# A fused attention and two feed-forward layers in one kernel: the first two blocks' loads, high parts and step order

## The chip, the cores and the metric

One Trainium2 chip, one core. The metric is the device time of one execution in microseconds; with several runs, their median. All operands come from HBM and the result goes back there. TensorE multiplies, VectorE and ScalarE do the elementwise work, GpSimd some of it, and SyncE issues the DMAs. "Local" and "strided" below are the two kinds of attention heads.

## The reference

Three stages, one behind the other, in fp32, over 2304 tokens (4 sequences of 576) and 512 channels:

```python
# attention: q, k, v are (4, 8, 576, 64); heads 0-3 local, heads 4-7 strided
rel = pos[:, None] - pos[None, :]
mask_local = (rel >= 0) & (rel < 32)
mask_strided = (rel >= 0) & (pos[None, :] % 32 == pos[:, None] % 32)
scores = where(mask, q @ k.T / 8, -1e9); attn = softmax(scores); out = attn @ v
# first feed-forward, w_in 512x2048, w_out 2048x512
h = x @ w_in; x = (h - tanh(h)) @ w_out
# second, w_gate and w_val 512x1536, w_out 1536x512
xn = x / sqrt(mean(x*x) + 1e-6) * rms_g
out = (silu(xn @ w_gate) * (xn @ w_val)) @ w_out
```

## The kernel before, in words

The tokens are cut into nine blocks of 256, gathered in five groups (two blocks, two, one, two, two). For a group the kernel computes the attention of its blocks and then the first feed-forward layer, 16 steps over f of 128 hidden channels each: a product with `w_in` (`pe_h`), tanh, a subtraction, and a product with `w_out` (`pe_x`) that is summed in PSUM. While a group's feed-forward runs, the attention of the next group is worked in between. The second feed-forward layer comes after all that.

Precise products take two parts of each operand: a high part, which is the value rounded for TensorE, and a low part, which is what is left. A product is then three matmuls. A weight of 128x512 arrives packed in 8-byte words and goes through four steps: `scale` (word **A** in the list below: ScalarE reads the raw weight), `merge` (**B**: two VectorE steps put the bits together), `high` (**P**: a cast, line 203) and `low` (**Q**: VectorE subtracts the high part). Weights are numbered in the order in which they are loaded: 0 is `in` 0, 1 is `in` 1, 2 is `out` 0, 3 is `in` 2, 4 is `out` 1; below they are in0, in1, out0, in2, out1.

The start, the attention of blocks 0 and 1 and the first three units of the feed-forward, is not left to the planner: the string `START` (line 25) lists every step by hand, and `first` (line 1212) issues them in that order. Each engine takes its own steps strictly in the order of the list; between engines only the data's semaphores order them. The words are these, with a block's number and L (local) or D (strided), and after it a half (0 or 1) or PSUM banks:

- the first word, after `<`: the loads, one letter each, issued on SyncE's queue in this order: t the table (a 128x544 tile: `ident16` and masks for the early blocks in columns 0 to 191, the identity in 192 to 319, masks of later blocks in 320 to 543), a and A the local queries and keys of block 0 and 1 (512 KB), b and B the strided ones (512 KB), c and C the local values (384 KB, on 96 partitions), d and D the strided values (256 KB), w the next weight (512 KB), 2 the loads of block 2;
- W9: nine products of zeros on TensorE at the very start;
- s: scores on TensorE, into two of the four banks x; m: row maxima on VectorE (line 447); e: exponentials on ScalarE (line 461); n: division by the sums on VectorE (lines 469 to 471); p: transposes on TensorE; c: their copy out of PSUM on ScalarE (line 487); v: the product with the values on TensorE; y: high part of the result on ScalarE (line 490); z: its low part on VectorE (line 494). So e1D0 is the exponentials of block 1, strided heads, half 0;
- h, T, G, I, J, X: a feed-forward unit: the product with `w_in` on TensorE, tanh on ScalarE, the subtraction on VectorE, the high part on ScalarE, the low part on VectorE, the product with `w_out` on TensorE. Unit 0 is f = 0 on block 0, unit 1 f = 1 on block 0, unit 2 f = 0 on block 1. h0 needs Q0 and all z of block 0; h1 needs Q1; h2 all z of block 1; X0 needs J0 and Q2.

Two tiles hold the output of A and two that of B, so a third weight's steps wait for the first's. The strided heads of blocks 0 and 1 take one transpose step and one copy (p0D, c0D) for both halves. What is not in the list is ordered by the planner, which places work by its own estimates of the times and may fill gaps with it; from the second group on the order on TensorE and SyncE is fixed by the program.

Of the kernel before, what the change touches and what calls it, by code (L numbers as in the profile page):

```python
# [22 lines left out]


START = """
<tabcdwABwCDwww2ww
W9 s0Lx m0L0 e0L0 m0L1 s0Dx n0L0 e0L1 m0D0 p0L0m1 m0D1 s1Lx A0 e0D0 B0 c0L0a n0L1 p0L1h1 P0 Q0 m1L0 m1L1 e0D1 c0L1a
v0Lh0 s1Dx n0D1 n0D0 A1 e1L0 p0Dh1 e1L1 y0L1 n1L0 m1D0 m1D1 c0Da n1L1 v0Dm0m1 y0L0 e1D0 y0D1 z0L0 y0D0 z0L1 p1L0h1
c1L0a B1 z0D0 P1 z0D1 p1L1h1 e1D1 c1L1a Q1 n1D0 n1D1 h0h0 A2 v1Lm1 T0 B2 A3 G0 y1L0 p1Dh1 c1Da y1L1 B3 v1Dh1m0 I0 P2
J0 y1D1 z1L0 y1D0 h1h0 T1 z1L1 z1D1 z1D0 P3 h2h1 Q2 G1 A4 Q3 T2 B4 I1 G2 J1 I2 J2 X0  # L30
"""


# [1 line left out]
def attn_moe_moe_kernel(  # L35
# [24 lines left out]
    nc = tc.nc  # L60
# [60 lines left out]
    tab = one.tile([128, 544], F32, name="tab")  # L121
# [27 lines left out]
    def mm(out_, lhsT, rhs, start, stop):  # L149
        nc.tensor.matmul(out_, lhsT, rhs, start=start, stop=stop, skip_group_check=True)  # L150
# [3 lines left out]
    def room_of(i):  # L154
        return (held, "v") if i >= 2 * FA - HELD else (wts, "w")

    class Weight:
# [40 lines left out]
            )  # L198
            self.b = t.bitcast(F32)

        def high(self, pool, tag):
            self.t = pool.tile([128, 2, 4, 128], F32R, tag=tag, name="w")
            nc.scalar.copy(out=self.t[:, 0].rearrange("p c f -> p (c f)"), in_=self.b)

        def low(self, eng):
            t = self.t.rearrange("p s c f -> p s (c f)")
# [40 lines left out]
    for f in range(1, FA):  # L247
# [3 lines left out]
    st1 = Stream(  # L251
        [w1[w] for w in w1_order],
        lambda i: room_of(i) + (nc.vector,),
        3, 2 * FA, lambda i: True,
    )
# [244 lines left out]
    class Local(Heads):  # L500
        w = 96
# [340 lines left out]
    def pe_h(g, f, a, e, bank=None):  # L842
        pool, tag = (ps_m, "m") if g == NG - 1 and f % 2 else (ps_h, "h")
        ps = bank("ps_h") if bank else pool.tile([128, 512], F32, tag=nth(tag, 2), name="ps_h")
        ps = ps[:, :e - a]
        w, x = w1["in", f].t, xs[g]
        seq = [(i, k, c) for c in range(4) for i, k in ((0, 0), (0, 1), (1, 0))]
        for n, (i, k, c) in enumerate(seq):
            mm(ps, w[:, i, c, :], x[:, k, c, a:e], n == 0, n == len(seq) - 1)
        h_of[g, f, a] = ps  # L850
# [326 lines left out]
    new_x(0)  # L1177
    new_x(1)

    def tab_load():  # L1180
        nc.sync.dma_start(out=tab, in_=tabs)

    units = [(0, f, 0, SUB) for f in range(LB)]
    for f in range(LB, FA):
# [3 lines left out]
    units += [(g, f, 0, width[g]) for g in range(1, NG) for f in range(FA)]  # L1188

    loads = {  # L1190
        "t": tab_load, "w": lambda: st1.load_to(st1.n + 1),
        **{c: o.load_qk for c, o in zip("aAbB", loc[:2] + strd[0] + strd[1])},
        **{c: o.load_v for c, o in zip("dD", strd[0] + strd[1])},
        **{c: (lambda o=o: o.load_v(0)) for c, o in zip("cC", loc[:2])},
# [6 lines left out]
    def bank_of(tags):  # L1201
        if tags == "x":
            return bank_x
        tags = [tags[k:k + 2] for k in range(0, len(tags), 2)]

        def bank(name):
            tag = tags.pop(0)
            return {"h": ps_h, "m": ps_m}[tag[0]].tile([128, 512], F32, tag=tag, name=name)

        return bank  # L1210

    def first(word):

        op, rest = word[0], word[1:]
        if op == "<":
            for c in rest:
                loads[c]()
        elif op == "W":
            z = att.tile([128, 512], F32, tag="sm", name="zero").bitcast(BF16)[:, :512]
            nc.vector.memset(z, 0.0)  # L1220
            ps = bank_of("m0")("ps_w")
            for _ in range(int(rest)):
                mm(ps, z[:, :128], z, True, True)
        elif op in "ABPQ":
            w = st1.ws[int(rest)]
            pool, tag, e = st1.place(int(rest))
            if op == "A":
                w.scale()
            elif op == "B":
                w.merge()  # L1230
                st1.i = int(rest) + 1
            elif op == "P":
                w.high(pool, tag)
            else:
                w.low(e)
        elif op == "h":
            pe_h(*first_units[int(rest[0])], bank_of(rest[1:]))
        elif op in "TGIJX":
            u = first_units[int(rest)]
            {"T": act_tanh, "G": dve_g, "I": g_hi, "J": g_lo, "X": pe_x}[op](*u)  # L1240
            if op == "J":
                xq.append(u)
            if op == "X":
                xq.remove(u)
        else:
            j, kind, rest = int(rest[0]), rest[1], rest[2:]
            o = loc[j] if kind == "L" else strd[j][0]
            fn = getattr(o, "st_" + op)
            if op in "sv":
                fn(bank_of(rest))  # L1250
            elif op == "p":
                i = 0 if o.fused else int(rest[0])
                fn(i, bank_of(rest if o.fused else rest[1:]))
            elif op == "c":
                fn(0 if o.fused else int(rest[0]), nc.scalar.copy)
            else:
                fn(int(rest))
# [23 lines left out]
    with tc.manual_schedule():  # L1281
        for word in START.split():
            first(word)
# [122 lines left out]
    for j in range(NJ):  # L1406
        for p in range(NP):
            first, last, end = (j, p) == (0, 0), p == NP - 1, (j, p) == (NJ - 1, NP - 1)
            me, nxt = pairs[p], pairs[(p + 1) % NP]
            st = Stage(j, p)  # L1410
# [132 lines left out]
```

## Time and profile before

| | us |
|---|---|
| median of 3 runs | 888.29 |
| lowest and highest | 886.44, 888.67 |
| the profiled execution, its own time | 887.14 |
| its span, first to last instruction | 885.3 |

The profile is of one execution. Its page gives each engine's busy time and the granted clock of TensorE; views by stretch, by engine in order of time and by line or tile show which instruction ran when, and behind it in brackets how long the engine had stood idle and what ended that. Starts are microseconds from the span's start. An instruction's time there may overlap the next one's by some 0.1 us, since the engines work in pipelines.

### The profile page before, as it was taken

How to read it: one execution, taken by the hardware profiler on the slowest of the kernel's cores; microseconds unless marked ns; L12 is line 12 of the kernel's file. 1: busy time of each engine (PE TensorE's matmuls, PEld its weight loads, DVE VectorE, ACT ScalarE, POOL GpSimd, SP SyncE). 2: the span in 40 equal slices, each digit the busy share in tenths (PEclk: the TensorE clock that was granted, in tenths of full speed). 3: DMA queues.
4: the chain of work that ended last, by engine and by line, in shares of the span. 5: the costliest groups of instructions: out<-in, count | busy, mean ns of one | idle time of the engine just before them, and what ended most of it. 6: DMA issues, size and time to landing. Idle time of an engine off the chain costs nothing.

```text
span 885.3 us, 14070 instructions
## 1 busy us (share of the span) xinstructions
PE 865.6 (98%) x5091; PEld 723.4 (82%) x5091; DVE 626.1 (71%) x1290; ACT 413.7 (47%) x916; POOL 247.6 (28%) x309
## 2 busy tenths in 40 slices
PE   7999999999999999999997999999999999999998
PEld 4888888888998887888887977888888888888886
DVE  5999778888779887657779845469688553435544
ACT  6887633323543333778657544533325324322230
POOL 0000057694366853000000449956200000000000
PEclk7999999999999999999999999999999999999999
DMA  9965224221313000889976889866661289544002
GB/s 302 367 221 180 76 75 157 98 63 36 116 55 110 25 19 26 330 311 366 412 262 226 302 304 410 329 239 214 212 216 48 82 315 348 182 147 140 1 1 95
DMA packets 63749, 164.12 MB, mean 185 GB/s; under 512 B 10112, under 2 KB 21760, under 8 KB 63680
## 3 DMA queue, kind: packets, MB, share of 16 engines
q1 hardware_dynamic: 62528, 162.18, 52.2%
q10 hardware_dynamic: 1152, 1.05, 0.3%
q8 instruction: 40, 0.66, 0.3%
q14 instruction: 29, 0.24, 0.1%
HBM read 119.16 MB, written 44.04 MB: 184 GB/s over the span
## 4 chain that ended last, share of the span: by engine, by line
PE 60%; DVE 9%; POOL 7%; issue 2%; DMA 2%; ACT 1%; ACTq 0%; SPq 0%; DVEq 0%; POOLq 0%
PE ps_pr L150 21%; PE ps_o L150 15%; PE ps_x L150 9%; PE ps_h L150 9%; POOL pr L674 5%; DVE so L714 4%; PE ps_q L150 4%; PE ps_m L150 1%; POOL pr L707 1%; DMA raw<-in_w_val_dram 1%; DVE tg L859 1%; DVE g L870 1%; DMA x2d<-xe 1%; DVE sm L450 0%; DMA sq<-in_q_str_dram 0%
## 5 line engine op out<-in xcount | busy, mean ns | idle before, releaser
L150 PE MATMUL ps_h<-xs,w 128*128 128x512 f32 (+1 forms) x984 | 214.3, 366 | 0.7 <-DVE tg L859 0.7
L150 PE MATMUL ps_x<-g,w 128*128 128x512 f32 (+1 forms) x984 | 214.1, 366 | 0.0
L150 PEld LDWEIGHTS ps_h<-xs,w 128*128 128x128 f32 x984 | 169.7, 190 | 30.5 <-DVE tg L859 1.2
L150 PEld LDWEIGHTS ps_x<-g,w 128*128 128x128 f32 x984 | 168.5, 189 | 30.3 <-ACT g L865 0.4
L150 PE MATMUL ps_pr<-xt,wt 128*128 128x512 f32 x576 | 137.0, 390 | 0.5 <-DVE s L1096 0.5
L150 PE MATMUL ps_o<-wt,p 128*128 128x512 f32 x576 | 135.9, 389 | 0.0
L150 PEld LDWEIGHTS ps_pr<-xt,wt 128*128 128x128 f32 x576 | 107.9, 188 | 23.6 <-DVE s L1096 0.9
L150 PEld LDWEIGHTS ps_o<-wt,p 128*128 128x128 f32 x576 | 108.1, 188 | 22.4
L674 POOL TENSOR_TENSOR pr<-sk,sq 128x256 f32<-128x256 f32 (+2 forms) x101 | 83.1, 857 | 132.2 <-DMA sq<-in_q_str_dram 127.8
L865 ACT CAST g<-tg 128x512 fp32r<-128x512 f32 (+1 forms) x82 | 46.5, 567 | 101.2 <-DVE tg L859 100.9
L1117 ACT COPY u<-ps_pr 128x512 f32<-128x512 f32 x72 | 41.9, 587 | 102.8 <-PE ps_pr L150 102.8
L707 POOL TENSOR_TENSOR pr<-sv,se 128x288 f32<-128x288 f32 (+12 forms) x104 | 69.7, 691 | 57.4 <-DVE so L714 19.8
L1169 DVE SCALAR_TENSOR_TENSOR osum<-ps_o,osum 128x512 f32<-128x512 f32 x80 | 54.8, 687 | 26.6 <-PE ps_o L150 25.9
L714 DVE TENSOR_REDUCE so<-pr 128x16 f32<-128x272 f32 (+11 forms) x104 | 64.8, 651 | 8.9 <-POOL pr L707 8.6
L302 POOL TENSOR_TENSOR ws<-wa 128x256 f32<-128x256 f32 x24 | 20.4, 872 | 179.6 <-DVE w L207 155.6
L150 PE MATMUL ps_pr<-xt,wo 128*128 128x512 f32 x288 | 67.4, 389 | 0.0
L150 PEld LDWEIGHTS ps_pr<-xt,wo 128*128 128x128 f32 x288 | 54.1, 188 | 11.2
L870 DVE TENSOR_TENSOR g<-tg,g 128x512 fp32r<-128x512 f32 (+1 forms) x82 | 55.2, 674 | 10.4 <-ACT g L865 9.8
L859 DVE SCALAR_TENSOR_TENSOR tg<-ps_h,tg 128x512 f32<-128x512 f32 (+1 forms) x82 | 50.5, 617 | 15.8 <-ACT tg L854 15.8
L196 DVE SCALAR_TENSOR_TENSOR ct<-ca,ct 128x512 uint32<-128x512 uint32 x68 | 47.5, 706 | 18.9 <-ACT ca L186 18.4
L854 ACT ACTIVATE tg<-ps_h 128x512 f32<-128x512 f32 (+1 forms) x82 | 44.2, 540 | 35.5 <-PE ps_h L150 35.4
L679 DVE TENSOR_REDUCE sc<-pr 128x4 f32<-128x256 f32 (+2 forms) x101 | 43.7, 436 | 12.1 <-POOL pr L674 11.6
(123 smaller groups left out, 1041.1 us busy)
## 6 DMA issues: line engine op xcount, KB each, us to landing
wt<-w SPq DMA_DIRECT2D x84, 512.0 KB, 4.6
w<-w SPq DMA_DIRECT2D x36, 512.0 KB, 6.2
raw<-in_w_out_dram SPq DMA_DIRECT2D x28, 512.0 KB, 6.1
w<-wo SPq DMA_DIRECT2D x24, 512.0 KB, 7.1
raw<-in_w_in_dram SPq DMA_DIRECT2D x16, 512.0 KB, 9.2
raw<-in_w_gate_dram SPq DMA_DIRECT2D x12, 512.0 KB, 7.0
raw<-in_w_val_dram SPq DMA_DIRECT2D x12, 512.0 KB, 7.4
v<-ct SPq DMA_DIRECT2D x24, 256.0 KB, 5.3
```

The costliest lines, as they stand in the source:

```text
L150: nc.tensor.matmul(out_, lhsT, rhs, start=start, stop=stop, skip_group_check=True)
L196: nc.vector.scalar_tensor_tensor(out=t, in0=self.a.bitcast(U32), scalar=3, in1=t, op0=ALU.logical_shift_left, op1=ALU.bitwise_or)
L674: nc.gpsimd.tensor_tensor(out=pr, in0=self.k[:, a:e, :], in1=self.q[:, c - c0:c - c0 + 1, :].to_broadcast([128, e - a, D]), op=ALU.mult,)
L679: pend.append(lambda: nc.vector.tensor_reduce(out=s[:, c - c0, a:e], in_=pr, axis=AX.X, op=ALU.add))
L707: nc.gpsimd.tensor_tensor(out=pr, in0=self.v[:, 0:c + 1, a:e], in1=self.e[:, c - c0, 0:c + 1].unsqueeze(2).to_broadcast([128, c + 1, e - a ...
L714: pend.append(lambda: nc.vector.tensor_reduce(out=o[:, c - g0, a:e], in_=pr.rearrange("l c d -> l d c"), axis=AX.X, op=ALU.add))
L854: nc.scalar.activation(out=t, in_=h_of[g, f, a], func=ACTF.Tanh, scale=WS)
L859: nc.vector.scalar_tensor_tensor(out=t, in0=h_of.pop((g, f, a)), scalar=WS, in1=t, op0=ALU.mult, op1=ALU.subtract)
L865: nc.scalar.copy(out=t[:, 0], in_=t_of[g, f, a])
L870: nc.vector.tensor_tensor(out=t[:, 1], in0=t_of.pop((g, f, a)), in1=t[:, 0].bitcast(F32), op=ALU.subtract)
L1117: nc.scalar.copy(out=u, in_=x[kd])
L1169: nc.vector.scalar_tensor_tensor(out=o, in0=ps, scalar=WS, in1=o, op0=ALU.mult, op1=ALU.add)
```

## The change

It touches the first two blocks alone. The table is loaded in two pieces, columns 0 to 319 (T) first and columns 320 to 543 (M) behind the first weight. The local queries and keys of block 1 (A) are loaded third instead of seventh, ahead of the strided ones of block 0 (b); the values of block 0 (c, d) move behind the first weight. The high parts (P) of the first four weights are cast by GpSimd instead of ScalarE; all later ones stay on ScalarE. The steps stand in another order throughout; some PSUM banks of transposes change with it (p0L0 takes m0, for one). The set of steps is the same.

```diff
 START = """
-<tabcdwABwCDwww2ww
-W9 s0Lx m0L0 e0L0 m0L1 s0Dx n0L0 e0L1 m0D0 p0L0m1 m0D1 s1Lx A0 e0D0 B0 c0L0a n0L1 p0L1h1 P0 Q0 m1L0 m1L1 e0D1 c0L1a
-v0Lh0 s1Dx n0D1 n0D0 A1 e1L0 p0Dh1 e1L1 y0L1 n1L0 m1D0 m1D1 c0Da n1L1 v0Dm0m1 y0L0 e1D0 y0D1 z0L0 y0D0 z0L1 p1L0h1
-c1L0a B1 z0D0 P1 z0D1 p1L1h1 e1D1 c1L1a Q1 n1D0 n1D1 h0h0 A2 v1Lm1 T0 B2 A3 G0 y1L0 p1Dh1 c1Da y1L1 B3 v1Dh1m0 I0 P2
-J0 y1D1 z1L0 y1D0 h1h0 T1 z1L1 z1D1 z1D0 P3 h2h1 Q2 G1 A4 Q3 T2 B4 I1 G2 J1 I2 J2 X0
+<TaAbwMcBdwCDwww2ww
+W9 s0Lx m0L1 m0L0 s0Dx e0L1 m0D0 e0L0 m0D1 n0L1 s1Lx A0 n0L0 p0L1m0 B0 e0D0 e0D1 m1L0 P0 s1Dx n0D0 c0L1a m1L1 p0L0m0
+A1 n0D1 Q0 e1L0 p0Dm1 B1 m1D0 c0L0a e1L1 c0Da A3 m1D1 n1L0 v0Lh0 P1 v0Dm0m1 e1D0 y0D0 y0D1 y0L1 p1L0h1 n1L1 z0D1 z0D0
+y0L0 e1D1 A2 p1L1m0 c1L0a z0L1 z0L0 n1D0 h0h0 c1L1a n1D1 T0 B2 G0 p1Dh1 c1Da v1Lm1 I0 Q1 y1L0 v1Dh1m0 J0 y1L1 P2 y1D0
+y1D1 B3 h1h0 z1L1 z1L0 P3 z1D0 z1D1 T1 Q2 A4 h2h1 G1 T2 Q3 B4 X0 G2 I1 I2 J1 J2
 """
@@ Weight.high
-        def high(self, pool, tag):
+        def high(self, pool, tag, copy=nc.scalar.copy):
             self.t = pool.tile([128, 2, 4, 128], F32R, tag=tag, name="w")
-            nc.scalar.copy(out=self.t[:, 0].rearrange("p c f -> p (c f)"), in_=self.b)
+            copy(out=self.t[:, 0].rearrange("p c f -> p (c f)"), in_=self.b)
@@ the table's load
-    def tab_load():
-        nc.sync.dma_start(out=tab, in_=tabs)
+    def tab_load(a, e):
+        nc.sync.dma_start(out=tab[:, a:e], in_=tabs[:, a:e])
@@ the loads by letter
-        "t": tab_load, "w": lambda: st1.load_to(st1.n + 1),
+        "T": lambda: tab_load(0, 320), "M": lambda: tab_load(320, 544), "w": lambda: st1.load_to(st1.n + 1),
@@ first
             elif op == "P":
-                w.high(pool, tag)
+                w.high(pool, tag, nc.gpsimd.tensor_copy)
```

## Rows read from the trace of the kernel before

**Rows 1.** The page, busy us, share of the span and instructions of TensorE
```profile
PE 865.6 (98%) x5091; PEld 723.4 (82%) x5091; DVE 626.1 (71%) x1290; ACT 413.7 (47%) x916; POOL 247.6 (28%) x309
```
**Rows 2.** Busy time by stretch; last three columns: clock, DMA share, GB/s
```profile
0.00:22.00 22.00, 16.13 (x253) 10.09 (x253) 11.96 (x47) 13.61 (x63) 0.54 (x8) 0.77 0.93 301
22.00:66.00 44.00, 42.08 (x417) 36.03 (x396) 41.87 (x123) 37.98 (x106) 0.00 (x0) 0.96 0.82 294
```
**Rows 3.** TensorE in order of time: start, us, instruction, idle before it
```profile
5.03 0.85 PE L150 MATMUL ps_s<-tab 128*128 128x384 bf16 x2
...
8.83 0.69 PE L150 MATMUL ps_s<-dq 64*64 64x64 f32 x32 [1.53 <-DMA dq<-in_near_d_dram]
...
13.54 1.56 PE L150 MATMUL ps_s<-lq 64*64 64x96 f32 x32 [0.87 <-DMA lq<-in_near_l_dram]
...
23.98 1.09 PE L482 MATMUL ps_p<-tab,sm 128*96 128x128 f32 x4 [1.25 <-ACT pT L487]
24.73 2.64 PE L150 MATMUL ps_h<-xs,w 128*128 128x256 f32 x12
...
30.49 1.70 PE L150 MATMUL ps_h<-xs,w 128*128 128x256 f32 x12
32.12 1.10 PE L150 MATMUL ps_s<-lq 64*64 64x96 f32 x26
33.15 1.70 PE L150 MATMUL ps_h<-xs,w 128*128 128x256 f32 x12
```
**Rows 4.** Busy time by stretch, that of h0 (columns as in the second group)
```profile
24.00:26.00 2.00, 2.00 (x10) 1.97 (x11) 1.93 (x6) 2.00 (x10) 0.00 (x0) 0.50 1.05 226
```
**Rows 5.** SyncE's issues in order of time, and single issues with us to landing
```profile
1.65 0.42 SPq L587 DMA_DIRECT2D dq<-in_near_d_dram  x1
...
3.76 0.79 SPq L519 DMA_DIRECT2D lq<-in_near_l_dram  x1
...
5.42 0.64 SPq L175 DMA_DIRECT2D raw<-in_w_in_dram  x1
...
10.94 0.38 SPq L175 DMA_DIRECT2D raw<-in_w_in_dram  x1
...
dq<-in_near_d_dram SPq DMA_DIRECT2D x1, 512.0 KB, 7.1
...
lq<-in_near_l_dram SPq DMA_DIRECT2D x1, 512.0 KB, 9.7
...
raw<-in_w_in_dram SPq DMA_DIRECT2D x1, 512.0 KB, 11.7
...
raw<-in_w_in_dram SPq DMA_DIRECT2D x1, 512.0 KB, 10.9
```
**Rows 6.** ScalarE in order of time: P0, A1, e1D0's first, y0D, T0
```profile
14.43 0.64 ACT L203 CAST w<-ct 128x512 fp32r<-128x512 f32 x1
...
17.16 0.67 ACT L186 ACTIVATE ca<-raw 128x512 f32<-128x512 f32 x1 [0.43 <-DMA raw<-in_w_in_dram]
...
21.25 0.38 ACT L461 ACTIVATE sm<-ps_s,nm 128x64 f32<-128x64 f32 x1
...
22.42 1.14 ACT L490 CAST xs<-ps_v 128x256 fp32r<-128x256 f32 x2
...
27.40 0.38 ACT L854 ACTIVATE tg<-ps_h 128x256 f32<-128x256 f32 x1 [0.61 <-PE ps_h L150]
```
**Rows 7.** VectorE in order of time: block 0's low parts, local and strided
```profile
22.10 0.75 DVE L494 TENSOR_TENSOR xs<-ps_v,xs 128x256 fp32r<-128x256 f32 x2
...
23.83 1.10 DVE L494 TENSOR_TENSOR xs<-ps_v,xs 128x256 fp32r<-128x256 f32 x2
```
**Rows 8.** One line (ns min/median/max), then groups by form, 505-625 and 625-800 us
```profile
L285 POOL CAST wo<-ws x24: 609/614/1126, 506.1 to 621.8; 128x512 fp32r<-128x512 f32 x24
...
L1101 DVE TENSOR_TENSOR p<-s,p 128x512 fp32r<-128x512 f32 x14 | 12.9, 921 | 5.4 <-ACT p L1100 5.0
...
L1101 DVE TENSOR_TENSOR p<-s,p 128x512 fp32r<-128x512 f32 x24 | 16.8, 702 | 7.3 <-ACT p L1100 6.6
```

## What I predict

> **What bounds the kernel now.** I read the page first, then busy time by stretch, then the first 37 us engine by engine. TensorE is busy for 98% of the span [rows 1], and its work is the same before and after, so the change can only be worth what TensorE loses at the start. The stretches say where that is: in the first 22 us TensorE is busy for 16.13, between 22 and 66 for 42.08 of 44 [rows 2]; of the latter's loss nearly all falls before 30.5 us. TensorE's own order shows the holes: the strided scores of block 0 wait 1.53 us for their queries and keys, block 1's local scores 0.87 us for theirs, the last local transposes 1.25 us for a copy on ScalarE; the first real product h0 starts at 24.73, the second, h1, at 30.49 and the third, h2, at 33.15, just behind 1.03 us of scores of a later group, put in as filler [rows 3]. From there TensorE has no hole. So the yardstick is the start of h2: what it moves, filler behind h1 included, the end moves. Part of the loss is clock: 12 products of 256 columns take 2.64 us in h0 and 1.70 in h1 [rows 3]; in h0's stretch the granted clock is 0.50, that is 1.2 of 2.4 GHz [rows 4], after a stretch in which TensorE mostly waited.
>
> What holds TensorE there is the chain behind it. VectorE is busy 11.96 us of the first 22 and 41.87 of the next 44 [rows 2]; ScalarE has no hole from 17.16 (0.43 us, for weight in1) to 27.40 (0.61 us, for h0) [rows 6]. ScalarE and VectorE, fed by loads that run one behind the other, decide when h0, h1 and h2 start.
>
> **Part 1: the loads.** Landing is issue plus time to landing [rows 5]: block 0's strided set 1.65 + 7.1 = 8.75; block 1's local set 3.76 + 9.7 = 13.46; in1 5.42 + 11.7 = 17.12; in2 10.94 + 10.9 = 21.84. The order changes only within the first nine loads. Block 1's local set, now third, lands no later than today's third (8.75), so the wait of 0.87 us goes. That buys less than it seems: these scores need PSUM banks that block 0's local scores free only when ScalarE has read both halves, about 11.0 (two exponential steps of 1.27 us behind 8.4; the 1.27 is worked out in part 3). Block 0's strided set becomes fourth. With 112 KB of table gone from the front (0.37 us at the 301 GB/s of [rows 2]) it could come at 8.4; a whole 512 KB load behind today's third it comes at 8.75 + 1.74 = 10.5. I take 8.4 to 10.5; both give the same h0 below. **The loads that matter later don't move**: in front of in1, and of in2, stand the same bytes as now (the table's second piece included). The loads run back to back, so I keep 17.1 and 21.84. The table's first piece is read at 5.03, behind the warm-up products and without a wait [rows 3]; it gains nothing there. Its second piece (masks) is first read by a later group's scores; it costs SyncE one more issue, about 0.4 us, in a queue that runs many microseconds ahead.
>
> **Part 2: high parts on GpSimd.** Four casts leave ScalarE, 0.64 us each, 0.52 to the next start [rows 6]. The same cast on GpSimd takes 0.61 (minimum and median), 1.13 at most [rows 8], and GpSimd is empty here. P0 and P1 are followed by other VectorE work before their low parts Q0 and Q1, so their latency is covered. But the ScalarE time they free lies ahead of waits: P0's 0.52 us ends up in the wait for in1, P1's in the wait for in2 (below). P2 and P3 come after h0, where ScalarE waits for TensorE now and then. Gain before h0: 0; behind it up to 0.5, in part 3's sum. What GpSimd's reading costs VectorE the trace shows elsewhere: VectorE's subtract of two tiles in SBUF takes 921 ns in the stretch in which GpSimd makes such casts (505 to 625 us) and 702 behind it [rows 8]. So 0.22 us for each cast that meets such a step; bounds 0 and one whole cast (0.61). Before h0 VectorE has a hole of some 3 us that hides it (by part 3 its step z0D1 waits until 24.5); on the path are P2 and P3. I take 0.1 us in all.
>
> The Trainium skill ("SBUF — State Buffer", section "Who interferes with whom") says more: a VectorE instruction with two SBUF inputs and a GpSimd instruction that reads SBUF exclude each other, and the second waits for the whole of the first. By it the four casts would cost VectorE up to 2.4 us (an estimate, four times the cast), half of it on the path; the 921 against 702 ns agree in direction and are far from a full stop each time.
>
> **Part 3: the order of the steps.** Merging block 0's maxima first (m0L1, m0L0, then e0L1) removes a wait of VectorE for ScalarE on the same bank, but VectorE then stands until the strided scores at 8.4 to 10.5. Two steps of ScalarE's new order count. A1 (weight in1) again waits for in1 until 17.1, now with c0L0 still behind it. And **A3 (weight in2) is moved from after h0 to before e1D0**; ScalarE takes its steps in order, so a wait in A3 holds up the exponentials of e1D0, the four copies y0 and everything behind them. ScalarE's arrival at A3: A1 runs from 17.16 for 0.67, 0.1 of it over the next step [rows 6], so e1L0 starts at 17.7. Today e1L0, two short copies y0L, e1L1 and c0D fill the time from there to e1D0 at 21.25 [rows 6]: 3.5 us, some 1.0 for the three copies and 1.27 for each exponential step. In the new order c0L0 stands in place of the y0L, which is as long: about 21.2. In2 lands at 21.84: wait 0.6 us.
> From there: A3 to 22.45 (0.6), e1D0 to 23.6 (21.25 to 22.42 today, 1.17 [rows 6]), two copies y0D to 24.45 (the pair takes 1.14, overlapping the next step by 0.3 [rows 6]). The low parts on VectorE follow, two strided at 1.10 and two local at 0.75 with overlap (about 1.0 and 0.7 to the next start) [rows 7]: to 26.3. h0 needs them all: **h0 at 26.4, against 24.73, 1.7 us later.** Today h0 starts while the last strided one is being written, since it reads the local ones first; the new order writes the local ones last.
> Behind h0 the new order gives back. h0 at the lower clock ends about 29.0 (2.64). T0 follows at once, then the copy c1D, where today A3 and a copy y1L0 stand between (0.6 and some 0.3): c1D 29.7 to 30.2, v1D to 31.1, **h1 at 31.2, against 30.49**. h1 ends at 32.8. The copies y1D (no P2 between them) end at 32.3, the low parts z1L and z1D, behind B3, at 33.6: **h2 at 33.7, against 33.15**; the gap behind h1 holds the same filler of about 1 us. With 0.1 for GpSimd: 0.6 to 0.7 us later.
>
> **Sum.** The profiled execution's own time is 887.14 (span 885.3 and 1.84 around it): 887.14 + 0.6 = 887.7. It lies 1.15 below the median of the runs (888.29), so I say **888.9**. A measurement here tells about 0.3% (2.7 us) from no change: I forecast no difference that can be told.
>
> **The rivals.**
> (a) *Loads come earlier.* If the new order loads faster (its small or 96-partition transfers lie elsewhere), in1 and in2 come 1.5 us earlier, ScalarE doesn't wait in A3, and h0 starts at 24.9, h1 at 29.7, h2 at 32.2: 0.9 earlier, **887.4**. For it: the rate of the first 22 us, 301 GB/s [rows 2], leaves room. Against: same bytes. The limit, with all loads there at 9 us, is h2 1.4 us earlier (ScalarE and TensorE then bind), **886.9**; with h0 at full clock as well (2.64 to 1.70 [rows 3]) **885.9**.
> (b) *Slower: the wait in A3 lowers the clock.* By part 3 TensorE stands some 3 us before p1L1 and h0, more than today. If p1D, v1L and v1D also run at 1.2 GHz, where today the clock is up before h1, their some 2 us take 1.55 times as long (h0 to h1 [rows 3]): h1 starts at 32.3 and, with the copies and low parts behind it, h2 at 34.6, 1.4 us later than today, **889.7**. If in2 also lands a microsecond later, all of it follows one for one: **890.7**. The point from which it decides: h0 is in2's landing plus 4.6, so it is late as soon as in2 lands after 20.1.
> (c) *GpSimd and VectorE block each other:* two to four casts with 0.3 to 0.6 on the path, 0.6 to 1.8 more, **889.5 to 890.7**.
> (d) *The start does what I say, but the planner, which orders the rest by its own times for the start, lays out the next stages otherwise.* VectorE is full up to 66 us [rows 2], so a worse or better order there shows: 2 us either way, **886.9 or 890.9**. That the change doesn't do what it says (block 1's set not early) is in it: by part 1 that changes nothing.
>
> **How the numbers follow.** Forecast 0.52, (a) 0.20, (b) 0.16, (c) 0.06, (d) 0.06. Over 0.3% faster, under 885.6, needs the limit of (a) and a good turn of (d): 0.07. Over 0.3% slower, above 890.95, needs the upper end of (b), (c) or (d): 0.13. Within: 0.80. The range runs from (a)'s limit with the clock, 885.9, to just past the upper ends of (b) and (c), 891.2.
>
> **What would show it.** Right: the third load landing by 8.8 and no wait at s1L for it; ScalarE idle at A1 and A3 until loads land at about 17 and 21.8; h0 later than 24.73, h1 and h2 within a microsecond of 30.49 and 33.15; casts on GpSimd of 0.6 to 1.1 us. Wrong: in2 landing before 20.5, with h0 no later than today; or a start as told and a difference that arises after 66 us.

## Result and profile after

| | runs | us, median (from, to) | profiled run, us | span, us |
|---|---|---|---|---|
| before | 6 | 888.38 (886.44, 889.30) | 887.14 | 885.3 |
| changed | 6 | 892.95 (890.99, 895.08) | 890.99 | 889.2 |

The changed kernel is slower: ratio 1.0055, 95% interval 1.0038 to 1.0071, some 4.9 us. I had forecast 888.9 in a range up to 891.2, and no difference that can be told. The profiled run of the changed kernel is the lowest of its six, so the two profiles show less of the difference (3.9 us) than the runs.

TensorE's work is the same 5091 instructions, busy 866.9 us where it was 865.6; the span grew by 3.9. The page's first part and the two stretches (us, then busy time and instructions of TensorE, its weight loads, VectorE, ScalarE and GpSimd, then the granted clock, DMA share, GB/s) answer to [rows 1, 2]:
```profile
PE 866.9 (97%) x5091; PEld 723.2 (81%) x5091; DVE 628.3 (71%) x1290; ACT 410.7 (46%) x912; POOL 249.6 (28%) x313
...
0.00:22.00 22.00, 13.86 (x189) 8.18 (x189) 12.56 (x49) 11.83 (x55) 1.76 (x10) 0.86 0.93 288
22.00:66.00 44.00, 41.92 (x455) 35.77 (x452) 39.23 (x117) 35.35 (x104) 1.23 (x2) 0.91 0.85 304
```
In the first 22 us TensorE does 189 instructions where it did 253. Where its time goes is seen in its order of time (start, us, instruction, idle before it and what ended it), which answers to [rows 3]:
```profile
8.87 0.95 PE L150 MATMUL ps_s<-dq 64*64 64x64 f32 x32 [1.85 <-DMA dq<-in_near_d_dram]
...
11.07 1.56 PE L150 MATMUL ps_s<-lq 64*64 64x96 f32 x32
...
20.30 1.98 PE L150 MATMUL ps_v<-pT,v 96*64 96x64 f32 x32 [2.58 <-ACT pT L487]
...
26.49 1.06 PE L482 MATMUL ps_p<-tab,sm 128*96 128x128 f32 x4 [2.08 <-DVE xs L494]
27.20 2.75 PE L150 MATMUL ps_h<-xs,w 128*128 128x256 f32 x12
...
32.19 1.70 PE L150 MATMUL ps_h<-xs,w 128*128 128x256 f32 x12
33.82 0.88 PE L150 MATMUL ps_s<-lq 64*64 64x96 f32 x16
34.62 1.69 PE L150 MATMUL ps_h<-xs,w 128*128 128x256 f32 x12
```
The wait for block 1's local set is gone (11.07). Two longer ones stand behind it, 2.58 us for a copy of ScalarE and 2.08 for low parts of VectorE, and h0, h1 and h2 start at 27.20, 32.19 and 34.62, that is 2.47, 1.70 and 1.47 later than before. ScalarE's order of time, which answers to [rows 6], says why: A1 stands 2.93 us for in1, with the copy c0L0 that TensorE needs behind it; A3 stands 0.46 us for in2, with e1D0 and the copies y0 behind it. T0 waits 1.63 for h0.
```profile
17.82 0.68 ACT L186 ACTIVATE ca<-raw 128x512 f32<-128x512 f32 x1 [2.93 <-DMA raw<-in_w_in_dram]
...
22.45 0.68 ACT L186 ACTIVATE ca<-raw 128x512 f32<-128x512 f32 x1 [0.46 <-DMA raw<-in_w_in_dram]
...
24.19 1.52 ACT L490 CAST xs<-ps_v 128x256 fp32r<-128x256 f32 x4
...
29.99 0.38 ACT L854 ACTIVATE tg<-ps_h 128x256 f32<-128x256 f32 x1 [1.63 <-PE ps_h L150]
```
VectorE's low parts, answering to [rows 7], stand for the copies, and the casts on GpSimd take the 0.61 of [rows 8]:
```profile
25.26 1.74 DVE L494 TENSOR_TENSOR xs<-ps_v,xs 128x256 fp32r<-128x256 f32 x4 [2.73 <-ACT xs L490]
...
14.11 0.61 POOL L203 CAST w<-ct 128x512 fp32r<-128x512 f32 x1 [13.05 <-DVE ct L196]
19.29 0.61 POOL L203 CAST w<-ct 128x512 fp32r<-128x512 f32 x1 [4.57 <-DVE ct L196]
```
The clock in h0's stretch and in h1's (columns as above), answering to [rows 4]: it is 1.2 GHz in h0, as before, and 2.4 in h1.
```profile
27.00:29.00 2.00, 2.00 (x11) 1.99 (x10) 1.76 (x8) 1.35 (x3) 0.00 (x0) 0.50 1.03 281
32.00:34.00 2.00, 2.00 (x44) 1.77 (x28) 1.97 (x6) 1.39 (x4) 0.61 (x1) 1.00 1.02 408
```
By h2 the start thus explains 1.5 of the 3.9 us between the two profiles (some 1.8 if the filler ahead of h2, 16 products here and 26 before, is counted as work). To see where the rest arises I counted TensorE's work from the two traces, each matmul at what its kind takes in before, and asked how much later the changed kernel reaches the same amount, in us. Between 40 and 130 us the two orders stand at different products, so no lag is given there:

| at | 34 | 130 | 300 | 560 | 700 | end |
|---|---|---|---|---|---|---|
| lag | 1.5 | 3.2 | 3.2 | 2.7 | 3.7 | 3.7 |

Between 40 and 130 us there are no new holes of TensorE to point at. What differs there is the order: the planner interleaves the next stages otherwise, TensorE's instructions up to about 130 us and VectorE's up to about 210. The last step of 1.05, between 620 and 640 us, is in every other kernel's profile as well against this one of before, also where the kernel measured as fast as before; it belongs to that one execution and not to the change.

### The profile page after: what moved, and what is told of

It reads as the page before. It is cut to its first block, busy times and chain, and to the rows that moved or that the text cites. A ratio compares the mean times of both kernels' runs of the same rounds, so it can differ in the third digit from the quotient of the medians.

```text
span 889.2 us, 14082 instructions
## 1 busy us (share of the span) xinstructions
PE 866.9 (97%) x5091; PEld 723.2 (81%) x5091; DVE 628.3 (71%) x1290; ACT 410.7 (46%) x912; POOL 249.6 (28%) x313
## 3 DMA queue, kind: packets, MB, share of 16 engines
q10 hardware_dynamic: 1152, 1.05, 0.4%
## 4 chain that ended last, share of the span: by engine, by line
PE 60%; DVE 6%; POOL 5%; DMA 4%; issue 2%; ACT 1%; SPq 0%; ACTq 0%; POOLq 0%; DVEq 0%
PE ps_pr L150 19%; PE ps_o L150 14%; PE ps_x L150 11%; PE ps_h L150 10%; POOL pr L674 4%; PE ps_q L150 3%; DVE so L714 3%; DMA wt<-w 2%; PE ps_m L150 2%; DMA x2d<-xe 1%; POOL pr L707 1%; DVE tg L859 1%; POOL ws L302 0%; DVE sm L450 0%; DMA sq<-in_q_str_dram 0%
## 5 line engine op out<-in xcount | busy, mean ns | idle before, releaser
L714 DVE TENSOR_REDUCE so<-pr 128x16 f32<-128x272 f32 (+11 forms) x104 | 65.8, 655 | 7.5 <-POOL pr L707 7.3
L859 DVE SCALAR_TENSOR_TENSOR tg<-ps_h,tg 128x512 f32<-128x512 f32 (+1 forms) x82 | 50.7, 619 | 16.2 <-ACT tg L854 16.0
```

The lines of the kernel that those rows point to most:

```text
L714: pend.append(lambda: nc.vector.tensor_reduce(out=o[:, c - g0, a:e], in_=pr.rearrange("l c d -> l d c"), axis=AX.X, op=ALU.add))
L859: nc.vector.scalar_tensor_tensor(out=t, in0=h_of.pop((g, f, a)), scalar=WS, in1=t, op0=ALU.mult, op1=ALU.subtract)
```

## The experiments

Theory 1: ScalarE's waits for weight loads in the start cost. Theory 2: the casts on GpSimd cost. Theory 3: the planner's order behind the start costs. Theory 4: the order of the loads costs. Ratios are against runs of the kernel before on the same chip, with 95% intervals. The kernels were run on several chips, on which the median of before lay between 886.78 and 888.38, so kernels are compared by their ratios. "h2" is its start in one profile each, and tells of that execution: with the same loads and steps it varies by some 2 us, as will be seen.

| kernel | us, median | ratio | h2 |
|---|---|---|---|
| changed | 892.95 | 1.0055 (1.0038, 1.0071) | 34.62 |
| e1 casts on ScalarE | 891.95 | 1.0048 (1.0032, 1.0065) | 34.18 |
| e4 loads of before | 892.08 | 1.0056 (1.0040, 1.0071) | 38.12 |
| e5 A3 late | 889.80 | 1.0033 (1.0018, 1.0049) | 32.37 |
| e7 A1, B1 and A3 late | 889.02 | 1.0019 (1.0003, 1.0036) | 30.93 |
| e12 as e7, Q3 and B4 exchanged | 888.94 | 1.0020 (1.0004, 1.0036) | 31.75 |
| e10 as e7, z1D0 and z1D1 exchanged | 887.51 | 0.9997 (0.9981, 1.0012) | 31.00 |
| e2 before, casts on GpSimd | 888.41 | 1.0012 (0.9996, 1.0027) | 33.77 |
| e3 before, new loads | 888.68 | 1.0019 (1.0005, 1.0033) | 34.23 |
| e9 as e3, A1 late | 887.39 | 1.0002 (0.9990, 1.0015) | 32.18 |
| e8 before, A1 late | 886.65 | 0.9998 (0.9984, 1.0012) | 30.37 |
| e14 before, z1D1 and z1D0 exchanged | 893.21 | 1.0063 (1.0043, 1.0083) | 31.02 |
| pin_before | 889.68 | 1.0029 (1.0013, 1.0045) | 31.39 |
| pin_after | 893.96 | 1.0071 (1.0048, 1.0093) | see below |
| pin_e7 | 888.67 | 1.0023 (1.0007, 1.0040) | see below |

**One part at a time.** e1 is the changed kernel with the casts back on ScalarE:
```diff
-                w.high(pool, tag, nc.gpsimd.tensor_copy)
+                w.high(pool, tag)
```


> The changed kernel with the four high parts back on ScalarE; on every other engine the order of all instructions is that of the changed kernel. Theory 1 (the start is late because ScalarE waits in A1 and A3 for loads, and TensorE's clock falls meanwhile): the casts are not what costs; P0 fits into the wait of A1, P1 delays e1D0 by 0.5 us, so h0 at 27.2 to 27.8 (27.20 with the casts on GpSimd) and h2 at 34.6 to 35.2, the total within 0.7 us of the changed kernel's 892.95 (ratio to before 1.0045 to 1.006). Theory 2 (GpSimd's casts block VectorE or come late): h0 and h2 at least 1 us earlier, total 891 or less. Theory 3 (the planner lays out the stages behind the start worse): no change either, since the layout behind is the same here.

891.95: nearly all of the loss stays, so theory 2 falls as the main cause. The ratio is 0.0007 below the changed kernel's, 0.6 us, which is inside the intervals. e2 does the casts alone, in before:
```diff
-                w.high(pool, tag)
+                w.high(pool, tag, nc.gpsimd.tensor_copy)
```


> The kernel before with only the four casts moved to GpSimd. Within the start theory 1 expects h0 at 24.7 (no change), h1 and h2 0 to 0.5 us earlier, and so 888.0 to 888.4 in total if the rest stays as it is. The planner lays out the next stages differently here, though (some 100 lines of TensorE's order differ). Theory 3: whatever the start does, the total moves by up to 2 us either way with that layout. Theory 2 (casts on GpSimd cost): h2 later than 33.6.

1.0012 with an interval that takes in 1. In its profile h0 starts at 24.19, 0.54 earlier than before, and the lag against before is +0.8 at 130 us: the planner gives this kernel another order as well, so even this plain edit doesn't test the casts alone.

e4 is the changed kernel with the loads in the order of before:
```diff
-<TaAbwMcBdwCDwww2ww
+<TMabcdwABwCDwww2ww
```


> The changed kernel with the loads in the order of the kernel before (the table still in two pieces, one behind the other); every engine but SyncE keeps the changed kernel's order. Theory 1 (order of the steps): block 1's local scores wait until about 13.5, in1 and in2 land at 17.1 and 21.8 instead of 17.8 and 22.4, h0 at 26.5 to 27.5, total 892 to 894. Theory 4 (the loads' order costs, by later in1 and in2): h0 back to 25.5 or earlier and the total to 890 or less.

Same time as the changed kernel, as theory 1 had it; its start is a miss. The profile shows one that is much worse than I expected (h0 at 29.44, h2 at 38.12: the new steps want block 1's local set early and wait for it, and A3 waits 2.24 us); that run, 894.76, is the slowest of its six, so I take from it only that the old loads don't mend the new steps. e3 is the opposite, the steps of before with the new loads:
```diff
-<tabcdwABwCDwww2ww
+<TaAbwMcBdwCDwww2ww
```


> The kernel before with only its loads in the changed kernel's order and the table in two pieces; VectorE, ScalarE and GpSimd keep their order, TensorE's differs in one piece of filler. Theory 1: the wait of 0.87 us ahead of block 1's local scores goes, in1 and in2 land within 1 us of 17.1 and 21.8; h0 at 24.3 to 25.0, total within 1 us of the kernel before (ratio 0.999 to 1.001). Theory 4 (the loads' order costs or gains by itself): 2 us or more either way.

1.0019, some 1.7 us, while VectorE, ScalarE and GpSimd keep the order of before to the end. ScalarE's order of time in this run shows the place:
```profile
17.47 0.67 ACT L186 ACTIVATE ca<-raw 128x512 f32<-128x512 f32 x1 [2.31 <-DMA raw<-in_w_in_dram]
```
A1 stands 2.31 us where it stood 0.43 [rows 6]: it arrives earlier, and the load comes no sooner. e9 takes this wait away by putting A1 behind c0D, and e8 does the same to before:
```diff
-... A1 e1L0 p0Dh1 e1L1 y0L1 n1L0 m1D0 m1D1 c0Da ...
+... e1L0 p0Dh1 e1L1 y0L1 n1L0 m1D0 m1D1 c0Da A1 ...
```


> The steps of before and the loads of the changed kernel (887.9 to 888.7 as the loads alone), with A1 moved as in e8. Theory 1: the loads cost only by the wait in front of A1, which in the run of the loads alone was 2.31 us; with A1 behind c0D at least 1 us of that comes back, ratio 0.999 to 1.0005, h0 at 23.5 to 24.5 where it was 25.05. Rival (the loads cost by themselves, as by the later landing of the far queries and keys): ratio stays at 1.0015 to 1.0025 and h0 at 25.

> The kernel before with one step moved: A1 (ScalarE's scaling of the second weight) from ahead of e1L0 to behind c0D; all orders behind the start stay those of before. Theory 1 (a wait of ScalarE for a weight load ahead of a step of the attention chain is paid in full): the 0.4 to 1.6 us by which that load is late, plus the 0.7 us of the step itself ahead of e1L0, come off the start: 885.2 to 886.4 beside 886.8, ratio 0.998 to 0.9995, h0 at 23.5 to 24.5. Rival (ScalarE's place in the start is covered by VectorE, and it is only the layout that costs): no difference, ratio 0.9995 to 1.001.

e9 is at 1.0002, so some 1.5 of the 1.7 us go with A1's place; the two intervals overlap, and theory 4 keeps nothing that can be told. e8 is a miss for theory 1: 0.9998, no difference. Its profile has h2 2.8 us earlier than before's, but that is not shown to be the edit's: the loads came early in this execution, so that TensorE starts the strided scores of block 0 at 6.30 without a wait, where [rows 3] has 8.83, and e14 below, with A1 in its old place, has h0 as early (22.55, here 22.91). A profile's h0 is at 1.2 or 2.4 GHz as it happens (here 2.4: the first 12 products take 1.68 us, where [rows 3] has 2.64). Moving A1 gained nothing that can be told where its wait had been 0.43 us, and some 1.5 us where it had been 2.31.

**The waits in the changed start.** e5 moves A3 alone behind T0; e7 also moves A1 behind c0D and B1 behind n1L0. All other orders are those of the changed kernel.
```diff
-A1 n0D1 Q0 e1L0 p0Dm1 B1 m1D0 c0L0a e1L1 c0Da A3 m1D1 n1L0 v0Lh0 P1 ...
+n0D1 Q0 e1L0 p0Dm1 m1D0 c0L0a e1L1 c0Da A1 m1D1 n1L0 B1 v0Lh0 P1 ...
-... T0 B2 G0 ...
+... T0 A3 B2 G0 ...
```


> The changed kernel with one step moved: A3 (ScalarE's first step of weight in2) from before e1D0 back to behind T0, where the kernel before has it; TensorE's, VectorE's and GpSimd's orders are the changed kernel's. Theory 1: the 0.46 us wait and A3's own 0.57 us leave the chain e1D0, y0, z0, so h0 at 26.0 to 26.3 instead of 27.20; behind h0 A3 now delays c1D by 0.57, so h1 0.4 to 0.6 earlier (31.6 to 31.8), h2 0.3 to 0.6 earlier, total 0.3 to 1 us below the changed kernel's 892.95. If A3's wait were the whole cost of the start: h2 back at 33.2 and total 891.5. Theory 3 (layout behind the start): the layout is unchanged, so at least 2 us over before remain, 890.4 or more.

> The changed kernel with A1 moved behind c0D, B1 behind n1L0 and A3 behind T0: ScalarE no longer stands in the queue for in1 or in2 ahead of the chain to h0; the other orders and the stages behind are the changed kernel's. Theory 1: h0 at 23.0 to 24.0, h2 at 31.0 to 32.2 (34.62 in the changed kernel), total 2.5 to 3.5 us below the changed kernel. Theory 3: some 2 us of layout remain, so the total is still about that of the kernel before (ratio 0.999 to 1.002) in spite of a start that is 1 to 2 us earlier. If the start were everything: 2 us below the kernel before.

e5 recovers 2.0 us of the 4.9 (1.0055 to 1.0033), more than the 0.3 to 1 I expected, and e7 3.2 (to 1.0019), as expected; the 1.2 between the two, for A1 and B1, is inside the intervals. ScalarE's and TensorE's order of time in e7:
```profile
19.51 0.72 ACT L186 ACTIVATE ca<-raw 128x512 f32<-128x512 f32 x1
...
23.82 0.72 ACT L186 ACTIVATE ca<-raw 128x512 f32<-128x512 f32 x1
...
26.22 0.67 ACT L186 ACTIVATE ca<-raw 128x512 f32<-128x512 f32 x1
```
```profile
24.25 1.66 PE L150 MATMUL ps_h<-xs,w 128*128 128x256 f32 x12
...
28.20 1.69 PE L150 MATMUL ps_h<-xs,w 128*128 128x256 f32 x12
...
30.93 1.69 PE L150 MATMUL ps_h<-xs,w 128*128 128x256 f32 x12
```
No wait for in1 or in2 is left, and h2 starts 2.2 us earlier than in the profile of before [rows 3]. Yet the kernel is 1.7 us slower than before. The 2.2 are no proof of a better start, though: that profile is one execution with a late start. pin_before and e14 below have the loads of before and its steps up to h0, and reach it at 23.50 and 22.55 where [rows 3] has 24.73. Whether the mended start is earlier has to be asked with the same order behind it.

**The start alone.** To compare starts with the same order behind them, I held TensorE's order in the stretch behind the start to that of the program, in three kernels; all engines then have the same order there.
```diff
-tc.manual_schedule(engines={mybir.EngineType.SP})
+tc.manual_schedule(engines={mybir.EngineType.PE, mybir.EngineType.SP})
```


> The kernel before with TensorE's order in the first group fixed as the program lists it, instead of laid out by the planner. Only there to stand beside the next run. Theory 3 (the layout of the stages behind the start moves the time): this alone moves the total by 1 to 3 us against the kernel before, either way. If layout matters little: within 0.7 us of it (ratio 0.999 to 1.001). Its start: h0 at 24.7, h2 without filler ahead, at 32.0 to 32.6.

> The changed kernel with the same order fixed: on TensorE, VectorE, ScalarE and GpSimd everything behind the start is then in the order of the run before this one, so the two differ by the start alone (the start's own order, the loads, the casts). Theory 1 (the start is late): 1.5 to 2.5 us above the run before this one, and h2 later by as much. Theory 3 (most of the 4.6 us comes from the layout behind): the rest of the 4.6 is missing here. If the start alone were the whole: 4 us or more between the two.

> The changed kernel with A1 behind c0D, B1 behind n1L0 and A3 behind T0, and TensorE's order outside the start held as in the two pinned kernels (889.68 with the start of before, 893.96 with the changed one), so that only the start differs. Theory 1 (in the start it is ScalarE's two waits for weights that cost): the mended start costs nothing against the start of before or gains up to 2 us, 887.7 to 890.2, with the third batch of W1 products (h2) at 31 to 32 us of the span. Rival (the new order of the attention steps, the casts or the loads cost by themselves): half or more of the 4.3 us stays, 892 to 894.

889.68, 893.96 and 888.67. By the ratios the changed start costs 3.7 us over that of before (1.0071 against 1.0029; by the medians 4.3), more than I had expected, and moving A1, B1 and A3 takes 4.3 back (1.0023; by the medians, which are of two chips, 5.3). That is all of it: between pin_before and pin_e7 no difference can be told, so the mended start is level with that of before. pin_before itself has the start of before and another order behind it, and is 1.0029 (1.0013, 1.0045): that order alone costs 2.6 us, as theory 3 had it. TensorE's order of time in pin_before, pin_after and pin_e7 (in the last two h1 and h2 run as one group of 24):
```profile
23.50 2.66 PE L150 MATMUL ps_h<-xs,w 128*128 128x256 f32 x12
...
31.39 1.66 PE L150 MATMUL ps_h<-xs,w 128*128 128x256 f32 x12 [0.41 <-DVE xs L494]
```
```profile
24.87 1.06 PE L482 MATMUL ps_p<-tab,sm 128*96 128x128 f32 x4 [3.61 <-DVE xs L494]
25.58 2.91 PE L150 MATMUL ps_h<-xs,w 128*128 128x256 f32 x12
...
31.20 3.52 PE L150 MATMUL ps_h<-xs,w 128*128 128x256 f32 x24
```
```profile
23.57 2.91 PE L150 MATMUL ps_h<-xs,w 128*128 128x256 f32 x12
...
29.69 3.17 PE L150 MATMUL ps_h<-xs,w 128*128 128x256 f32 x24
```
In pin_after TensorE stands 3.61 us for the low parts of block 0; h0 is 2.1 later than in pin_before. ScalarE's order of time there shows that it is A3 that holds it: in1 came early in this execution, and the wait stands in A3.
```profile
14.70 0.66 ACT L186 ACTIVATE ca<-raw 128x512 f32<-128x512 f32 x1 [0.83 <-DMA raw<-in_w_in_dram]
...
20.86 0.66 ACT L186 ACTIVATE ca<-raw 128x512 f32<-128x512 f32 x1 [1.99 <-DMA raw<-in_w_in_dram]
```
In all four profiles with A3 ahead of e1D0, whenever in2 came, h0 follows A3's start by about the same time: 4.75 us (changed), 4.72 (pin_after), 4.72 (e4) and 5.22 (e1).

The lag between pin_before's and pin_after's profiles is 1.7 at 34 us and still 1.8 at 160. Later it grows to 3.4 with the same order of instructions, in steps at 200 to 250 us (0.7) and 520 to 560 us (0.9); what ties those to the start I haven't settled.

**The order behind the start.** Two neighbouring VectorE steps exchanged leave the start as it is and make the planner lay out the next stages otherwise. e14 does it in before, e10 and e12 in e7:
```diff
-... z1L1 z1D1 z1D0 P3 ...
+... z1L1 z1D0 z1D1 P3 ...
```
```diff
-... z1D0 z1D1 T1 ...
+... z1D1 z1D0 T1 ...
```
```diff
-... Q3 B4 X0 ...
+... B4 Q3 X0 ...
```


> The kernel before with the two neighbouring VectorE steps z1D1 and z1D0 exchanged: the start is the same but for that, and the planner's order of the next stages differs (TensorE in some 60 places, VectorE in some 95, up to about 100 us). Theory 3 (the planner's order behind the start is worth microseconds by itself, and the order of before is a lucky one): 0.7 to 3 us slower, ratio 1.001 to 1.0035, with h2 within 0.5 us of before's. Rival (the order behind the start is worth nothing, what the changed kernel lost is all in its start): 0.9990 to 1.0010.

> The changed kernel with A1, B1 and A3 late (e7, 889.02, ratio 1.0019) and the neighbouring steps Q3 and B4 exchanged near the end of the start: another order behind it (TensorE in some 70 places against e7). Theory 3: the time moves by 0.7 us or more from e7's, either way, 886 to 891. Rival (that order is worth nothing): 888.4 to 889.6 as e7.

> As e12, with z1D0 and z1D1 exchanged in place of Q3 and B4: a third order behind the same start (TensorE in some 40 places against e7, VectorE in some 20). Theory 3: by the smaller number of places less than in e12, 887.5 to 890.5. Rival: 888.4 to 889.6 as e7.

e14 loses 0.63%, 5.6 us, more than the whole change and more than theory 3 allowed. Its h2 is 2.1 us earlier than before's, outside the 0.5 I expected, by loads that came earlier in this execution: A1 starts at 14.99 and waits for nothing. e10 gains 2.0 us on e7 and comes level with before; the two intervals overlap, so this gain is the less certain. e12 is no different from e7, a miss for theory 3, though it moves more places than e10. So the order behind the start cost up to 5.6 us against that of before, and no order tried was better than that one by more than its interval.

The traces tell the worth of the order apart from the execution's start. By 130 us TensorE has done the same work in all kernels, so I take the lag against before at 130 us less the lag at h2, with the filler ahead of h2 counted as work. It is 1.3 to 1.4 us in the changed kernel and in e1, e4, e5 and e7, which all have TensorE's order of the changed kernel behind the start, and 1.3 in e12. It is 0.1 in e10, 0.2 in e2, at most 0.1 in e3, e8 and e9, which keep the order of before up to there, 1.7 to 1.8 in the three pinned kernels, and 2.7 in e14. Five executions of one order agree within 0.1 us while their starts differ by up to 7: this part of the loss belongs to the order. In the changed kernel it lies in no hole of TensorE; where it lies I haven't settled.

TensorE's order of time in e14 shows one place where it is paid:
```profile
208.26 4.33 PE L150 MATMUL ps_h<-xs,w 128*128 128x512 f32 x12 [2.04 <-DVE tg L859]
```
VectorE's order of time there: the product L859 that TensorE needs stands behind a row of sums of another stage (L714) and a scaling (L471).
```profile
205.30 1.09 DVE L714 TENSOR_REDUCE so<-pr 128x21 f32<-128x231 f32 x2
206.31 0.70 DVE L471 TENSOR_TENSOR sm<-sm,ss 128x384 f32<-128x384 f32 x1
206.94 0.67 DVE L714 TENSOR_REDUCE so<-pr 128x21 f32<-128x252 f32 x1
207.53 0.68 DVE L859 SCALAR_TENSOR_TENSOR tg<-ps_h,tg 128x512 f32<-128x512 f32 x1
```
Busy time in this stretch, in e14 and then in before (columns as above):
```profile
205.00:210.00 5.00, 2.96 (x13) 2.09 (x12) 4.86 (x9) 1.12 (x2) 2.59 (x4) 0.97 0.00 0
210.00:215.00 5.00, 5.00 (x22) 3.99 (x20) 2.09 (x5) 2.80 (x5) 0.00 (x0) 0.69 0.00 0
```
```profile
205.00:210.00 5.00, 5.00 (x28) 4.21 (x27) 4.06 (x10) 1.24 (x4) 3.04 (x5) 1.00 0.12 44
210.00:215.00 5.00, 5.00 (x24) 4.12 (x23) 4.06 (x8) 1.57 (x5) 3.04 (x5) 1.00 0.01 3
```
TensorE is busy 2.96 of 5 us, the clock then falls (mean 0.69 from 210 to 215), and the lag against before grows by 3.3 us at a hole of 2.04. Before has no hole there. The 2.7 us ahead of 130 us hold two more waits of TensorE, of 0.54 and 0.75 between 100 and 120 us; before has neither. The profiled run, at 892.35, is like the others of e14: all six lie between 891.54 and 894.63.

## Why the prediction was wrong

**Part 1, the loads: right as far as it went, with one term taken as fixed that is not.** The third load landed by 7.5 and the wait for it went, without gain. "Block 0's strided set at 8.4 to 10.5": 8.82. A1 found in1 at 17.82, not 17.1, and A3 in2 at 22.45, not 21.84. That half microsecond is not shown to come from the new order: of one order of loads in1 comes at different times in different runs. A1 ended its wait for it at 14.70 (pin_after), 16.20 (e5), 16.40 (e1), 17.47 (e3) and 17.82 (changed) with the new order, and at 15.90 (pin_before) and 17.16 (before) with the old one; in e14, with the old one, in1 was there by 14.99. I had taken one landing of one run as a constant, and it was a late one.

**Part 2, the casts: right in what the runs can tell.** 0.61 us each, and 0.6 us in all, inside the interval (e1). My 0.1 us for what they cost VectorE is not measured by any run. The exclusion that the Trainium skill ("SBUF — State Buffer", section "Who interferes with whom") describes would have made 2.4 us of them (an estimate, four times the cast); the changed kernel does not test it, since its casts met no VectorE step with two inputs in SBUF: during the first two VectorE reads maxima out of PSUM (L447) and small tiles, during the third it stands idle, and during the fourth it reads one operand from PSUM (L494).

**Part 3, the steps: the mechanism right, the size too small.** This is the step that failed in the start. A1 and A3 are where ScalarE stood, as I said. Behind A3 my working holds almost step by step: from A3's start to h0 4.75 us where I had 4.55, from h0 to h1 4.99 (4.8), from h1 to h2 2.43 (2.5). But A3 started 0.6 later than the 21.85 of the sum, and h2 came at 34.62, 1.47 later than before where I had 0.55. The later in2 is the second half of rival (b), which I had given 0.16. Its other half, that p1D, v1L and v1D run at 1.2 GHz, did not come: they took 0.60, 1.15 and 0.86 us, where before has 0.66, 1.15 and 0.86. And the start from which I counted, that of one profile of before, was itself late: h0 at 24.73 where the same start reaches it at 23.50 and 22.55 in other executions. The runs put the changed start's cost at 3.2 us (changed against e7) to 3.7 (pinned kernels), where I had 0.6 to 0.7.

**The yardstick failed.** "What [h2] moves, the end moves" holds only with the same order behind h2. The profiled executions of e7 and e14 have h2 more than 2 us earlier than that of before, and end 2.3 and 5.3 us later (spans 887.6 and 890.6 against 885.3; 1.05 of it is the step between 620 and 640 us). "From there TensorE has no hole" is true of the trace of before up to 231.88 us, where it stands 0.70 us, and it is no property of the kernel: it holds for the order that the planner found there. That is rival (d), which I gave 0.06 and 2 us. For this change it is worth 1.3 us by the traces (h2 to 130 us) and 1.7 by the runs (what is left in e7), which the exchange in e10 makes good; for another order it was 5.6. That the forecast left the order out of its sum is the second step that failed.

**Sum.** By the ratios: ScalarE's waits for in1 and in2 in the start 3.2 us (changed against e7) to 4.3 (pin_after against pin_e7); the order behind the start 1.7 (e7 against before) to 2.0 (e7 against e10); casts and loads by themselves too little to tell. 3.2 and 1.7 add to the 4.9 by construction; the pinned kernels (3.7 to 4.3 for the start) and the traces (1.3 for the order up to 130 us) measure the two apart and agree within the intervals. How much of the 3.2 is A1's wait and how much A3's is not settled: A3 alone gives 2.0 (e5). No kernel tried here is faster than before by more than its interval; e8 (0.9998) and e10 (0.9997) are level with it.

## What to carry to other kernels

In an engine that takes its steps in order, don't put a step that waits for a load ahead of one on the critical chain unless the load lands with some 3 us to spare; here the end of one wait for one load lay anywhere from 14.70 to 17.82 us. Don't read the worth of an edit at the start from one profile on each side either: the start of the same kernel varied by 2 us between executions. Where a planner lays out what follows, a small exchange of steps may cost more than the edit to be measured: hold that order, or try several, before a difference of half a per cent is put down to the edit. And a bottleneck engine without holes in one trace is no proof that it will have none, or take as long, with another order behind the same start.

## What the runs showed of the hardware

A wait of TensorE in the midst of full work can cost more than its length: 2.04 us at 206 us in e14 were followed by a stretch at a mean clock of 0.69, and the lag grew by 3.3. In e12's profile, a run at 892.69 where its median is 888.94, a wait of 2.66 us for ScalarE near 428 us did the same:
```profile
430.63 10.04 PE L150 MATMUL ps_x<-g,w 128*128 128x512 f32 x36 [2.66 <-ACT g L865]
```
There the lag against e7's profile grew by some 4.2. By then all engines' orders are those of e7, whose profile has no such wait and does these 36 products in 8.46 us; so it is a thing of that execution. Other profiles have it at the same place: 1.92 us in e1's, the slowest of its six runs, where the 36 products behind it take 10.07 us and the lag grows by 3.5. In pin_before's and e2's it is 1.28 and 1.45 us, and the products behind it take 8.46 and 8.48: there it cost its length alone. It is part of the 3 to 7 us by which the runs of one kernel differ here.
